# A short convolution with two taps per product in one more channel group, in a fused attention and long-convolution kernel

## The chip, the cores and the metric

The kernel runs on one core of a Trainium2 chip. A core has a matrix engine (TensorE, PE in the profile, with its weight loads as PEld), a vector engine (VectorE, DVE), a scalar engine (ScalarE, ACT), a general engine (GpSimd, POOL) and a synchronisation engine that here issues most of the DMA transfers (SyncE, SP). The metric is the device time of one execution in microseconds.

## The reference

Two independent parts are computed and laid side by side along the last axis: columns 0 to 575 are part A, columns 576 to 1151 are part B. The inputs are bf16, the sequence has 2048 positions and the width is 576.

Part A is attention with a compressive memory: 32 heads of 18 dimensions, 4 segments of 512 positions.

```
for s in range(4):
    logits = einsum('bhqd,bhkd->bhqk', qs, ks) * scale + mask
    a_dot  = softmax(logits) @ vs
    pq     = phi(qs)                      # t + 1 for t > 0, else exp(t)
    a_mem  = (pq @ M) / (pq @ z + 1e-6)
    o      = g * a_mem + (1 - g) * a_dot
    M, z   = M + phi(ks)^T vs, z + sum(phi(ks))
out_a = concat(o) @ wo
```

Part B is a short convolution of k with four taps per channel, a product with v, a long convolution of 2048 positions per channel (by an FFT of 4096 points), a skip term and a product with q.

```
k_shift[s] = sum over i in 0..3 of k[s - i] * shift_k[:, i]
kv         = k_shift * v
y          = irfft(rfft(kv) * rfft(ssm_k)) + kv * ssm_D
out_b      = q * y
```

## The kernel before, in words

**Tiling of part B.** The 576 channels go through in five groups of 128, 128, 128, 128 and 64. The four full groups begin at channels 0, 128, 256 and 384; the last loads channels 448 to 575 and uses the upper 64 of them. For a group, k and v are loaded transposed from HBM (kT, vT: channels on the partitions, 2048 positions along the row, 16 zero columns ahead of k; lines 421 and 424, tag X4 with two slots, X_0 and X_1 in the rows). The four taps of a channel become entries of diagonal weights: `dgf` (lines 432 to 442) builds them, the tile is dg.

For groups 0 to 3 a chunk of 512 positions takes four products of 128x128 weights, one for each tap, each on kT shifted by that many columns and summed in PSUM (`c4`, lines 467 to 470, by way of line 142). For the group in `PAIRED`, which is group 4 alone, one product takes two taps: 64 partitions hold the channels, the other 64 hold the same channels shifted by one position, and the weights have two diagonals of 64 under each other, 128x64. Two such products on the two halves of the columns of the matrix engine make a pair (`cm`, lines 472 to 485, by way of line 144). For group 4 the shifted rows come from one DMA within the tile (`kc4`, line 447), and one more DMA lays the second half of v below the first (`vc`, line 450). VectorE multiplies the PSUM result with v (line 492), a DMA stores it to HBM (kvst, line 498), and the long convolution loads it later in another layout (xsx, line 526): two transform stages, a pointwise product (lines 601 and 606), the inverse, a transposing DMA (zt, line 634), a last stage, the product with q (line 661, tile q, which has one slot) and the output store (line 668).

**Part A.** For every segment the projections of q and k are stored to HBM by DMA (qd, line 1005) and loaded back in an order of 32 rows for each head (pad, line 1019). For every group of four heads there are up to three score products (s0, s1, s2; line 1222), an exponential on ScalarE over 1024 columns at a time (line 1229), a mask on GpSimd (line 1236), the product with v (av), and a passage through HBM (ad, line 1287; am, line 1330) to the memory term and the output projection (stores at line 1379).

**What sets the order.** The work is cut into 1348 named steps (1350 after the change). Three tables, TURN, ENGINE and SLOT, say in what order all steps are issued, on which engine each runs, and which buffer each tile takes; `plan()` decodes them (lines 1412 to 1429), and the loop at lines 1505 and 1506 issues the steps one by one. Each engine goes through its own part of that order strictly in turn: a step that waits holds back everything behind it on the same engine. DMAs are issued from SyncE's queue, a few from ScalarE's. Copies out of PSUM run on ScalarE (line 148) or VectorE (line 150), as the table ENGINE says.

Names as they occur below: conv3.00, conv3.01, conv3.10 and conv3.11 are the four chunks of group 3; kT3 and vT3 its loads; s0_4 is the first score product of the heads' group 4 (the groups of all segments counted through); pad1.0 is the first load of padded rows of segment 1.

Of the kernel before, what the change touches and what calls it, by code (L numbers as in the profile page):

```python
# [1411 lines left out]
def plan(prm=PRM):  # L1412
# [25 lines left out]
    "bQFFBGoBvQAIAUYErgAJAXQECgFLBGwBTARvAXEBbgFqBL4AawBwAfYAUQRSBDwA9AB+AQYA+AD3AKIBBAE9AAEB+QALAVkEWgRNBKQBBgEFAYcBPgA/AAIBBwEYAQMBTgRAABkBGgFCABQBQQBDAB"
    "YAigEVARYB0wBbBAwBRAANARsBdQR7BHYErwBcBNQAEAFrBGwE9QB8BH8BEQESAW0EEwFwBBcBcQRPBFAERQBHACIBcgRzBHcEeAQjASQBeQR6BEYAiAGjAW4EHgEcASABpQEfAV0EbwQdAbAEcwE8"
    "ASEB1wAbACUBbAB1AQ4B2ACJAQ8BXgRyAD0BPgE/AUgASgBmAIMBLgEmATABLwFyAZUESQAnAUsAKgFMAHQBgAGWBIsBTQAsASsBTgBHBIwBMgEzATQBSAR6AdkAOAFSAHwBTwBQAI4B2gB7AW0AjQ"  # L1440
    "E6ATkBVgRVBDUBMQF9AX8EbgA7AYAEXwQpASgBjwEtAY0ElwSYBNsAbwBAATYBSQFgBI4EhAFRAEEBNwHFAcYBQgHHAX0EngFDAVcEfgSTAaABpgRMAVMAggTBAXcBlAHCAcMBlwGBBFgEVABiBJUB"
    "VQCFBNsBmQGbAXkBhgR2AdwB3QGdAVIByQFEAcsBygGWAXgB3gGfAZoBgQGYAU8BoQHTAZwBSAFGAUoByAG1BEsBTQG2BMwB1AHEAY8EUwJSAs0B1QGQBM4BkQFWAM8BVwC3BNAB0QFRAVgAswS4BN"
    "YBtASaBOkBWQBOAUUB0gHqAdcBUwGnBFAB7QHrAUcBYQRWAZAB7wGSAe4BYwGmAbEEZAFXAdgBpwGFAd8BmQThAbIE4AFjBFQCVAGHBKgBiARVAeMBVgLwAVUCWAGpAVcC5AGsBOIB7AHlAagE5gGu"
    "BKoErQSCAakEuQFkBKsErwTnAWUEAwLxAegBBALyAewEmwSDBKoBrQH0AYoEBQKcBIQE/QFYAv8BiQRaApEEugH+AdkB8wEHAlkCCQJbAskECAJZAWkC9QGGAQACXgFaAa4BygSrAV8B9wHiBGAB9g"
    "GvAbYBZgRhAfkBrAFnBGUBkgRbAXIC+wHaAWYBXAH4AQoCuQS6BPoBwQTCBLABLwJoAnQCcQIGAgsC/AEXAnMCwwQMAsQEGAIZAosEAQJ1AiECiQIiAgICIwK7AYwEaARhAr0BEwINAosCvAFjAsYE"
    "FQKxAWkEsgFdAl8C4wR2AhQCDwJcApMEXgIQAm0CHQIRAmoCXQEOArMBngQrArcBYAIkApQEFgIaAh8CHgK4AcUEywTRBGICvgEgAhIC0gTMBHcCegK/AXgCMwIlArkCGwJ5AiYCHAInAigCugLoBO"
    "kEuwKlAowCtAHAAbsEewKOArUBvQKEArwEvwJkAqsChgJlAp0EfAK+AoECjQKtAmYCZwKsAikC5gR+An0CgwKfBI8CrwKxArAC5wSFAoAChwLkBDsCggIqAn8CvgSuAuUEswIsApAC6gSIArQCkQI3"
    "ArUCbgLrBL0EpwKyAtMEOgLxBIoCPAI8A9QE8gS2Au0ELQI9A+4EkwKSAqAEtwLAArwCoQS4AsUCawIyAqQCHgU0Aj0CNQJsAscCxgKaAr8EyQLABMgC8wTKAm8CwQIuAssCwgL0BPUEMALNAvYENg"
    "LPAjgCzAI/AzkCzgJBA9MClALVAtQCPgOiBNACMQLvBKMEzQRCA/AEmwLXAmIBowJaAEADQwJFApwCRAKlBEQDRgLRAtYCXAPZAtgC7QJNAlIDxAKXApUCwwJDA84EZwHSAlsDTgJdA+8ClgLuAkUD"
    "XwPnAukC6AJOA/cE/QRTA9oC8AL4BNsC/gTPBHACpARQA9wC3gLQBKYCXgPHBPEC8wKgAvICRwKYAkYDYAPIBJkCSAPjAk8C6gLkAtUEUAL6BNYEYQMkBd0CRwP/BOUC3wJiA08DAAX0AuEC4AINBU"  # L1450
    "kD4gJRA/UC/QIOBdsE5gKdAkAC9gJBAtcE/wL+AlQD2gT5BPkC6wLYBOwC+wJIAgED+gKhAgIF2QRJAmMDAwMCA2gDogJXAz4CSgM/AgsDngINA2sDTANKAgADDAOfAgcDZwNtA/cCGQP4AmoDaQMB"
    "BQkDSwIIA2wDBAOoAvwCDgOpAg8FCgNlAwcFJQUFAw8DCAUQBSYFBgNkAxADmgPcBGYDqgLdBJwDcwObAxIDEQNuA40DbwNwA3UDcQN6Ax0DWAOWA5gDFQN7Ax8FcgMTA0sDIQMlA30DdAOSA5cDmQ"
    "N3A5QDfANRAgMFTQN5A0ICBAWTA6QDGAN2AxoDVQOdA6YDpQOVA6ADFAOiA3gDHAMWAxsDBQUeA6cDVgOEAxcDngMiBaEDnwMGBSADtAMiAyMFJAMfA/sEtQMmA6MDIwO2A7ADJwP8BLEDIAWoA94E"
# [83 lines left out]
```

## Time and profile before

| | |
|---|---|
| runs | 276.62, 283.88, 286.04 us; median 283.88 |
| profiled execution | 278.62 us, span 276.9 us, mean granted TensorE clock 0.993 |
| TensorE products | 256.1 us busy, 92% of the span |
| VectorE | 235.3 us, 85% |
| ScalarE | 233.9 us, 84% |
| GpSimd | 186.7 us, 67% |
| DMA | 53.96 MB, mean 195 GB/s |

A busy share is an average over the span. The stretches at the beginning and the end have other limits than the middle, so the shares are read together with the table by stretches. A DMA share over 1 in such a table means that the packets of several transfers overlap on the engines. Where a timeline puts several instructions in one row, it gives the start of the first, the time from it to the end of the last, and their count; a few records of products are missing, so a count may be one short.

### The profile page before, as it was taken

Reading aid. Unit: us, or ns where it says so; the run is one execution under the profiler, and the core shown is the slowest. Engines: PE = TensorE matmul, PEld = TensorE weight load, DVE = VectorE, ACT = ScalarE, POOL = GpSimd, SP = SyncE. Lnnn points to the kernel's source line nnn. Section 1 sums busy time; section 2 is a strip of 40 time slices with the busy share of each in tenths; the row PEclk is TensorE's granted clock in tenths of the full one; section 3 lists DMA queues with packets and bytes.
Section 4 is the critical chain, followed back from the end, with each engine's and each line's share of the span. In section 5 each row is a group of like instructions: output and inputs, shape, how many; then the busy total and the mean of one; then the engine's idle time right before and its main releaser. Section 6 shows DMA issues by size and latency. Waiting matters only on the chain. (4 is left out here: it accounts for less than half of the span.)

```text
span 276.9 us, 9623 instructions
## 1 busy us (share of the span) xinstructions
PE 256.1 (92%) x3950; PEld 159.9 (58%) x3961; DVE 235.3 (85%) x380; ACT 233.9 (84%) x293; POOL 186.7 (67%) x266
## 2 busy tenths in 40 slices
PE   5898999999899999999999799999999999789991
PEld 2554666655645666666556466556557665555670
DVE  7788679899999999987989799986898898779942
ACT  4867778888987898989999799999999999799830
POOL 7169324538998968346857799758776499969600
PEclk9999999999999999999999999999999999999997
DMA  6997999998999797997967998688995755586674
GB/s 191 214 160 164 220 241 283 204 217 202 222 190 250 239 179 200 182 241 148 254 156 150 248 203 206 137 213 254 217 208 153 230 179 132 163 196 151 153 134 110
DMA packets 136293, 53.96 MB, mean 195 GB/s; under 512 B 116360, under 2 KB 128952, under 8 KB 136250
## 3 DMA queue, kind: packets, MB, share of 16 engines
q1 hardware_dynamic: 134506, 52.45, 84.6%
q10 hardware_dynamic: 1744, 0.90, 1.2%
q8 instruction: 31, 0.51, 0.8%
q14 instruction: 12, 0.10, 0.1%
HBM read 22.18 MB, written 17.50 MB: 143 GB/s over the span
## 5 line engine op out<-in xcount | busy, mean ns | idle before, releaser
L1229 ACT ACTIVATE P<-PS 128x1024 bf16<-128x1024 f32 x160 | 153.8, 1032 | 14.4 <-PE PS L1222 13.2
L1236 POOL TENSOR_SCALAR_AFFINE_SELECT P<-P 128x512 bf16<-128x512 bf16 (+1 forms) x112 | 80.7, 741 | 53.0 <-ACT P L1229 42.9
L601 POOL TENSOR_TENSOR PQ<-X,Hx 128x256 bf16<-128x256 bf16 x72 | 49.7, 721 | 7.9 <-PE PS L144 4.1
L1222 PE MATMUL PS<-pad 25*128 25x384 bf16 (+6 forms) x512 | 36.5, 300 | 4.0 <-DMA pad<-qk_scratch 1.9
L150 DVE CAST A<-PS 128x1024 bf16<-128x1024 f32 x21 | 25.2, 1218 | 2.4 <-PE PS L144 2.2
L142 PE MATMUL PS<-xT,wk 128*126 128x512 bf16 (+1 forms) x100 | 25.4, 384 | 0.0
L1222 PEld LDWEIGHTS <-pad 25*128 25x128 bf16 (+1 forms) x512 | 11.1, 91 | 24.1 <-issue 17.7
L144 PE MATMUL PS<-P,V 128*32 128x256 bf16 (+3 forms) x512 | 22.9, 302 | 1.3 <-POOL P L1236 1.0
L142 PE MATMUL PS<-xT,wq 128*126 128x512 bf16 (+1 forms) x95 | 24.0, 383 | 0.0
L150 DVE CAST dn<-PS 126x512 bf16<-126x512 f32 (+1 forms) x29 | 19.7, 684 | 4.9 <-DMA qk_scratch<-dn 2.1
L144 PEld LDWEIGHTS <-Ft 128*64 128x64 bf16 x704 | 19.6, 110 | 7.0 <-issue 6.3
L142 PE MATMUL PS<-wv,xT 128*128 128x288 bf16 x160 | 23.5, 287 | 0.0
L142 PE MATMUL PS<-wo,am 126*128 126x288 bf16 (+1 forms) x144 | 22.4, 287 | 1.0 <-ACT P L1229 1.0
L144 PE MATMUL PS<-W,xs 128*64 128x128 bf16 x576 | 21.1, 220 | 1.5 <-ACT P L1229 0.4
L144 PE MATMUL PS<-A,Ft 128*64 128x128 bf16 (+1 forms) x640 | 22.1, 216 | 0.3 <-DVE dn L150 0.2
L144 PEld LDWEIGHTS <-xs 128*64 128x64 bf16 x576 | 18.0, 109 | 6.2 <-issue 5.2
L144 PE MATMUL PS<-G,PQ 64*128 64x128 bf16 (+1 forms) x640 | 20.7, 217 | 0.7 <-ACT P L1229 0.3
L1035 POOL TENSOR_SCALAR f<-dn 126x512 bf16<-126x512 bf16 (+2 forms) x7 | 17.6, 2520 | 4.5 <-ACT dn L148 2.2
L144 PEld LDWEIGHTS <-PQ 64*128 64x128 bf16 (+1 forms) x640 | 18.3, 97 | 3.8 <-issue 2.9
L150 DVE CAST Z<-PS 128x1024 bf16<-128x1024 f32 x13 | 15.9, 1223 | 4.4 <-PE PS L144 2.8
L142 PEld LDWEIGHTS <-xT 128*128 128x128 bf16 x160 | 14.6, 98 | 7.0 <-issue 2.4
L150 DVE CAST X<-PS 128x1024 bf16<-128x1024 f32 x14 | 17.1, 1222 | 1.7 <-PE PS L144 1.2
(165 smaller groups left out, 454.6 us busy)
## 6 DMA issues: line engine op xcount, KB each, us to landing
pad<-qk_scratch SPq DMA_DIRECT2D x15, 512.0 KB
a_scratch<-ou SPq DMA_DIRECT2D x15, 256.0 KB
qk_scratch<-dn SPq DMA_DIRECT2D x15, 252.0 KB
xs<-in_B_ssm_k_dram SPq DMA_DIRECT2D x4, 512.0 KB
kv_scratch<-X SPq DMA_DIRECT2D x4, 512.0 KB
xs<-kv_scratch SPq DMA_DIRECT2D x4, 512.0 KB
q<-in_B_q_dram SPq DMA_DIRECT2D x8, 256.0 KB
out_dram<-q SPq DMA_DIRECT2D x8, 256.0 KB
```

Of the source, the lines that this page charges most:

```text
L142: self.nc.tensor.matmul(out, lhsT=lhsT, rhs=rhs, start=start, stop=stop)
L144: self.nc.tensor.matmul(out, lhsT=lhsT, rhs=rhs, start=start, stop=stop, tile_position=pos)
L150: self.nc.vector.tensor_copy(out=out, in_=in_)
L601: self.nc.gpsimd.tensor_tensor(out=self.t(Pt)[:, 1024 * ri + 256 * k:1024 * ri + 256 * k + 256], in0=a[:, 256 * h:256 * h + 256], in1=self ...
L1035: eng.tensor_scalar(out=self.t(fm)[0:M, ws, :], in0=self.t(dense[m])[0:M, ws, :], scalar1=0.0, scalar2=1.0, op0=ALU.max, op1=ALU.add)
L1222: nc.tensor.matmul(o, lhsT=t[r, 1, q0:q0 + P], rhs=t[r, 0, q0:L], start=True, stop=True, tile_position=(32 * j, 0))
L1229: self.nc.scalar.activation(out=out2(jj), in_=self.psf(pso[jj]), func=ACT.Exp, scale=scale)
L1236: self.nc.gpsimd.affine_select(out=ap, in_=ap, compare_op=ALU.is_ge, fill=0.0, base=0, pattern=pat + [[1, P]], channel_multiplier=-1)
```

## The change

Group 3 (channels 384 to 511) is put into the paired form. It has 128 channels, not 64, so each half of 64 channels needs its own two rows of partitions: for channels 384 to 447 the shifted rows are copied into the upper 64 partitions of kT itself, and for channels 448 to 511, which stood there, both the rows and the shifted rows are first copied into a spare tile, k2, that takes the one slot of tag q. That is two DMAs (kb3, lines 456 and 457) and then one (kc3, line 460), and the second step may not start until the first has read its source. A chunk of 512 positions then takes four products of 128x64 weights, two by two on the two halves of the columns. The code for it is there in the kernel before; the set of groups selects it:

```diff
-PAIRED = (4,)
+PAIRED = (3, 4)
```

The three tables are replaced as a whole. One line of each stands for the rest:

```diff
 TURN = (
-    "AABzAHcAXQACABwAaQADAHUAewB2AIQAYgABAGUAXgBhAIUAjQBkAIcAWwBfAIkAeABjAIsAeQBgAGoAdAAEAAgABQCIAIYAaACMAI4AigAJAB4AXAAfAKkACgAhAAsApQCnAKYADACrAA0AqAAOAI"
...
+    "AABjAGAAdQCGAAEAfQB5AB4AegADAI8AjQCLAAIAXgAEAB8ACABfAGEAZACHAIkAewAFAGoAXQBrACEAIgCIAAkAHAB8AHgAIAAjAI4AdgCQAIoAjABiAAoAbAALAGUAggANAB0AZgCRAJcArQCrAK"
...
```

There are as many weight loads and products on TensorE as before. Some 86 steps change between ScalarE and VectorE, in about equal numbers both ways, and 32 between GpSimd and VectorE. Four loads of attention weights go from ScalarE's queue to SyncE's; one load of weights and two output stores go the other way. SyncE issues four more DMAs in all.

In TensorE's order conv3.00 stood ahead of the score products s1_6 and s0_6 before; it now stands directly behind s0_6, and s2_6 comes between the second and the third chunk. The load pad1.0 stood 68 steps ahead of its reader s1_8 in the whole order and now stands 38 ahead; the load of padded rows for segment 2, pad2.0, stood 33 ahead of its reader s0_17 and now stands 56 ahead.

SyncE's queue from the key load of group 3 to pad1.0, before (X_0 is kT, X_1 is vT; qk_scratch<-dn is a store of projected q and k, a_scratch<-ou and am<-a_scratch belong to the attention's passage through HBM, wo is a weight load):

```order
42 L421 DMA_TRANSPOSE X_0_101<-in_B_k_dram 128x2048
43 L424 DMA_TRANSPOSE X_1_102<-in_B_v_dram 128x2048
44 L526 DMA xs_106<-kv_scratch 128x32x64
45 L1287 DMA a_scratch<-ou_150 128x2x512
46 L1294 DMA cs_157<-ou_150 32x1x128
47 L697 DMA wo<-in_A_wo_dram 126x4x576
48 L1019 DMA pad_123<-qk_scratch_164 128x2x1024
```

and the same stretch of the changed kernel:

```order
42 L421 DMA_TRANSPOSE X_0_101<-in_B_k_dram 128x2048
43 L424 DMA_TRANSPOSE X_1_102<-in_B_v_dram 128x2048
44 L1005 DMA qk_scratch_164<-dn_117 14x9x1024
45 L456 DMA q_104<-X_0_101 64x2048
46 L457 DMA q_104<-X_0_101 64x2048
47 L1005 DMA qk_scratch_164<-dn_116 14x9x1024
48 L1287 DMA a_scratch<-ou_150 128x2x512
49 L1330 DMA am_136<-a_scratch 126x1x512
50 L460 DMA X_0_101<-X_0_101 64x2063
51 L526 DMA xs_105<-in_B_ssm_k_dram 128x32x64
52 L1294 DMA cs_157<-ou_150 32x1x128
53 L1019 DMA pad_123<-qk_scratch_164 128x2x1024
```

The three copies stand behind the value load, with two stores and a load of the attention between the two copies into the spare tile and the one in place; the weight load of wo has gone further back.

ScalarE's queue at the beginning, up to the first exponential (Ft are the tables of the transform, pad and dn the projections of q and k, V those of v, fe the phi of the attention's memory), before:

```order
28 L336 ACTIVATE Ft<-xs_105 128x16x64
29 L148 CAST pad_123<-PS 128x512 x2
30 L148 CAST dn_117<-PS 126x512
31 L336 ACTIVATE Ft<-xs_105 128x16x64
32 L148 CAST V_125<-PS 128x16x2x9
33 L1041 ACT_TABLE_LOAD
34 L1041 ACTIVATE fe_156<-dn_116 126x512
35 L1229 ACTIVATE P_1_132<-PS 128x1024 x2
```

and after the change:

```order
23 L336 ACTIVATE Ft<-xs_105 128x16x64
24 L148 CAST pad_123<-PS 128x512
25 L336 ACTIVATE Ft<-xs_105 128x16x64
26 L1229 ACT_TABLE_LOAD
27 L1229 ACTIVATE P_1_132<-PS 128x1024
28 L1041 ACTIVATE fe_156<-dn_116 126x512
29 L1229 ACTIVATE P_1_132<-PS 128x1024
```

The cast of V and the phi have left the place ahead of the first exponential.

SyncE's queue at the end, from the last transposing load (CT<-Z), before:

```order
191 L634 DMA_TRANSPOSE CT_100<-Z_103 128x32x64
192 L1379 DMA out_dram<-oA_152 128x576
193 L643 DMA q_104<-in_B_q_dram 64x16x64 x2
194 L1379 DMA out_dram<-f_118 128x576
195 L1379 DMA out_dram<-f_119 128x576
196 L1379 DMA out_dram<-oA_151 128x576
197 L668 DMA out_dram<-q_104 64x16x64 x2
198 L1379 DMA out_dram<-f_122 128x576
```

and after the change:

```order
195 L634 DMA_TRANSPOSE CT_100<-Z_103 128x32x64
196 L1379 DMA out_dram<-oA_153 128x576
197 L643 DMA q_104<-in_B_q_dram 64x16x64
198 L1379 DMA out_dram<-oA_152 128x576
199 L1379 DMA out_dram<-oA_151 128x576
200 L643 DMA q_104<-in_B_q_dram 64x16x64
201 L1379 DMA out_dram<-f_121 128x576
202 L1379 DMA out_dram<-f_122 128x576
203 L668 DMA out_dram<-q_104 64x16x64 x2
```

The second q load now has two output stores between it and the first, and no output store of part A stands behind the last stores of part B.

## Rows read from the trace of the kernel before

**Rows 1.** The page, first part: busy us, share of the span, instructions of each engine.

```profile
PE 256.1 (92%) x3950; PEld 159.9 (58%) x3961; DVE 235.3 (85%) x380; ACT 233.9 (84%) x293; POOL 186.7 (67%) x266
```

**Rows 2.** Busy time by stretch; after ACT and POOL: granted clock, DMA share, GB/s.

```profile
0.00:10.00 10.00, 6.14 (x34) 3.17 (x35) 7.88 (x36) 5.99 (x18) 5.03 (x14) 1.00 0.82 216
...
70.00:90.00 20.00, 19.22 (x311) 11.72 (x310) 18.74 (x26) 17.63 (x19) 18.80 (x30) 1.00 1.04 222
...
260.00:277.00 17.00, 10.96 (x116) 7.30 (x115) 8.18 (x15) 4.34 (x10) 2.16 (x4) 0.89 0.63 126
```

**Rows 3.** TensorE's timeline at group 3: start, length, operation, count, idle time before.

```profile
78.69 1.90 PE L142 MATMUL PS<-X,dg 128*128 128x512 bf16 x7
80.52 0.56 PE L1222 MATMUL PS<-pad 25*128 25x384 bf16 x8
...
83.46 0.68 PE L1222 MATMUL PS<-pad 25*128 25x512 bf16 x4
84.30 1.68 PE L142 MATMUL PS<-X,dg 128*128 128x512 bf16 x7 [0.16 <-issue]
85.91 1.07 PE L144 MATMUL PS<-G,PQ 64*128 64x128 bf16 x32
```

**Rows 4.** TensorE's timeline at group 4, which has the paired form.

```profile
108.29 0.62 PE L144 MATMUL PS<-X,dg 128*64 128x512 bf16 x4
108.84 0.41 PE L1222 MATMUL PS<-pad 25*128 25x512 bf16 x4
```

**Rows 5.** SyncE's timeline around the loads of group 3 and the copy of group 4.

```profile
68.84 0.83 SPq L1005 DMA_DIRECT2D qk_scratch<-dn  x1
69.77 4.08 SPq L421 DMA_TRANSPOSE X<-in_B_k_dram  x1
73.96 2.91 SPq L424 DMA_TRANSPOSE X<-in_B_v_dram  x1
...
81.47 0.39 SPq L1019 DMA_DIRECT2D pad<-qk_scratch  x1
...
102.97 0.55 SPq L447 DMA_DIRECT2D X<-X  x1
```

**Rows 6.** Weight loads from the tile of diagonals: ns shortest/median/longest.

```profile
L142 PEld LDWEIGHTS <-dg x64: 95/98/102, 19.1 to 85.4; 128*128 128x128 bf16 x64
...
L144 PEld LDWEIGHTS <-dg x8: 106/106/109, 108.3 to 110.3; 128*64 128x64 bf16 x8
```

**Rows 7.** DMA in the stretch 102 to 108 us, with the issues in it.

```profile
DMA packets 4326, 1.30 MB, mean 216 GB/s; under 512 B 3974, under 2 KB 4170, under 8 KB 4325
...
X<-X SPq DMA_DIRECT2D x1, 257.9 KB
```

**Rows 8.** TensorE's timeline at the score products s0_4 and s1_8.

```profile
69.12 0.60 PE L1222 MATMUL PS<-pad 25*128 25x512 bf16 x4
...
95.16 0.40 PE L1222 MATMUL PS<-pad 25*128 25x384 bf16 x8
```

**Rows 9.** Timelines of SyncE and TensorE at pad2.0 and its reader.

```profile
148.95 0.59 SPq L1019 DMA_DIRECT2D pad<-qk_scratch  x1
...
153.91 0.40 PE L1222 MATMUL PS<-pad 25*128 25x512 bf16 x4 [1.55 <-DMA pad<-qk_scratch]
```

**Rows 10.** The chain that ended last (start, us, what), and SyncE's last issue.

```profile
264.68 0.65 SPq L1379
...
266.18 4.14 DMA q<-in_B_q_dram
...
273.14 0.63 SPq L1379 DMA_DIRECT2D out_dram<-f  x1
```

**Rows 11.** ScalarE's timeline ahead of the first exponential.

```profile
22.34 1.06 ACT L336 ACTIVATE Ft<-xs 128x1024 bf16<-128x1024 int32 x1 [2.23 <-DVE xs L331]
23.31 0.42 ACT L148 CAST V<-PS 128x288 bf16<-128x288 f32 x1
...
25.04 0.63 ACT L1041 ACTIVATE fe<-dn 126x512 bf16<-126x512 bf16 x1
```

More of the change, by code (lines that the diff above doesn't have):

```diff
@@ L1438 @@
[L1438 to L1453, printed above, removed]
@@ new lines @@
+ENGINE = (
+    "AwICAwIBAgMDAgECAQMCAQIBAAIAAgIAAQACAgMEBAQCBAQCAAIAAgACAAIEBAQCAAIAAgACAAIEBAQDAAIAAgACAAIEBAQDBAQAAgACAAIAAgQEBAIEBAACAAIEBAEEAgQEAQIEBAIEBAIDAQQCAA"
+    "ECAwMDAwAAAAAAAAAAAAAAAAQEBAQEAAIAAQABAAEAAQACAAABAgAAAQIAAAICAAACAgQEBAQAAQABAAEAAgQEBAIBAgIBAgIBAgIBAgMBAgAAAgIAAAIBAAACAgAAAgIAAgABAAIAAgACAAIDAAEB"
+    "AwABAQMAAQEDAAEAAQEDAAEBAwACBAQAAQEDAAEBAwABAQMAAgABAQMAAQEDAAIEBAABAQMAAQEDAAEBAwACAAEBAwABAQMAAQQEAAEBAwABAQMAAQEDAAIAAQEDAAEBAwACBAQCAAQCAAQCAAQCAA"
+    "QCAAQCAAIAAgQAAgACBAACAAIEAAIAAgQEBAAAAQEAAAECAAACAgAAAgEAAAICBAQEBAQEBAQEAwECAgECAwECAwECAgECAAABAgAAAgIAAAIBAAACAgACBAQEAAIEAAIEAAIEAAIEAAIEBAQEBAAC"
+    "AwABAQMAAQEDAAEBAwACAAEBAwABAQMAAgQEAAEBAwABAQMAAQEDAAEAAQEDAAEBAwACBAQAAQEDAAEBAwABAQMAAgABAQMAAQEDAAEEBAABAQMAAQEDAAEBAwACAAEBAwABAQMAAgQEAgAEAgMABA"
+    "ICAAQCAwAEAgIABAICAAIAAgQAAgABBAACAAIEAAEAAQQEBAAAAQIAAAIBAAACAgAAAgIAAAECBAQEBAQEBAQEAgECAgECAgECAgECAgECAAACAgAAAQIAAAICAAACAQACBAQEAAIEAAIEAAIEAAIE"
+    "AAIEBAQEBAACAwABAQMAAQEDAAEBAwACAAEBAwABAQMAAgQEAAEBAwABAQMAAQEDAAIAAQEDAAEBAwACBAQAAQEDAAEBAwABAQMAAQABAQMAAQEDAAIEBAABAQMAAQEDAAEBAwABAAEBAwABAQMAAg"
+    "QEAgAEAgIABAIDAAQCAwAEAgMABAICAAEAAgQAAgACBAACAAIEAAIAAgQEBAAAAgIAAAECAAABAgAAAgIAAAICBAQEBAQEBAQEAgECAgECAwECAgECAgECAAACAgAAAgEAAAIBAAABAQACBAQEAAIE"
+    "AAIEAAIEAAIEAAIDAAEAAQABAQMAAQEDAAEBAwACAAEBAwABAQMAAQQEAAEBAwABAQMAAQEDAAIAAQEDAAEBAwACBAQAAQEDAAEBAwABAQMAAgABAQMAAQEDAAIEBAABAQMAAQEDAAEBAwABAAIAAg"
+    "ABAQMAAQEDAAEAAgACAgIABAICAAQCAwAEAgIABAIDAAABAAABBAAAAQAAAgEAAAIAAAEEAAACAAABAQQCAAEAAQACAAEEAAIAAQABAAIAAQACAwIAAgABAAICAgACAAIAAgICAAIAAgACAwIAAQQE"
+    "BAACAAIEBAQCAAIAAgABAAIEAAEAAgABAAIAAQABAwMAAgACAAEDAwACAAIAAQICAAIAAgABAwMAAgQEBAACAAIEBAQCAAIAAgABAAIEAAEAAgABAAIAAQABAwMAAQACAAECAwACAAIAAgMDAAIAAQ"
+    "ABAgIAAgQEBAACAAIEBAQCAAEAAQACAAIEAAEAAgACAAIAAgABAwIAAgACAAICAgACAAIAAQMCAAIAAgABAwIAAgQEBAACAAIEBAQCAAIAAQQAAgABAAIAAgMCAAEAAQABAAICAgABAAEEBAQAAgQE")
@@ new lines @@
+SLOT = (
+    "AAEAAAEAAAAGAAAAAQAEAAEFAAEAAgYHBgABAAMCBgcAAQAABQQFBAEAAAIDAQQABAUBAQIAAgAAAgMHAAYABwUEAwYAAwAABwEEBAACAwEEAAABAgMBAAEAAAIAAQAEAAMABQEBAgIFAwMAAQACBg"
+    "AGBwEABgIGAQQABAQGAgMAAAYDBAIAAgAABgIEAAAGAAMBAQAEBAQAAQQCBgECBgICBAAAAAIGBAACAwcAAgAEAgIGAAMBAQIEBAYEAQAAAAUAAgEDAgIEBQMDAAIBAAQAAgADAQEAAgADAwECAAAB"
+    "BgAGAAEAAAEAAQIAAQADAAAABAABAAQDAQcGAgIBBAYHAAAAAAEBAQUBAwcABAAAAgYABAQCAgIGAAQAAwQABgAAAAYEAwECAAEEAAMAAgQCAQQAAgAGAAIABAICBAQCAAMAAQQAAQQAAAECAAMEAA"
+    "IGAgACAAACBAYEAQMAAAYBBwADAgADAAQEAAcAAgIEAQAFAQYABgAGBwEGAQAHBgEGAQACAAEAAQIAAQAEAAMAAAACAQADAAIDAwAHAgEGAAAABAcBAgYBAwEAAAcBAQAAAgYEAAQAAQAEBAYBBAAC"
+    "BgIDAQAEAgAGBAECBAIGAAIGAwYEBAQAAgQABAMCBgEFAQIEAAQAAgYCAAIEAAAGAgEGAAAEBAYEAwcAAAQBAgADAgQDBgQAAgADAAICAQMCAQcAAAEBAAABBwAHAQAGAQEGAAEAAQIABAABAAMAAA"
+    "AHBAMHAQEGAAYCAgAHAAABAgIBAQEAAwEABAMBAAEABAEGAgIAAQIEAgQAAAUBAAQEBAIDAgEGBAAEAgICAAEDAAQGBAAGAwAEAAECBAACAAIGAQIEBAYEAwIEAAICAAAABgEFAAMAAAMCBgQDBgIE"
+    "AgAAAQcBAAAAAAEBAAQDAAIAAwYAAAYDBAIHAgEBBAEGAgAAAgAEBgAEAQYAAAAABgAEAQEEAAEEAAECBgIEAQEGAAAGBgEGAQAAAgAEAAIGBAQBBgABBAACAgIAAQIEAAQBAAYCAAABAAYAAAQEAA"
+    "QABgACAQQBBAIGBgIEAQAAAAIABAABAgIBAAAAAgYAAgEAAgAAAgYBAAACBAYABgECAAYCAgYAAQAAAAEEAQAABgAGAQECBAEAAAAGAAACBAEGAQYAAgAEBAEEAQECAAQGAgYAAAYAAAAE")
```

50 lines of the change are left out of this document (23 added, 27 removed).

## The prediction

> **What bounds the kernel now.** I began with the page's first part: TensorE is busy 256.1 us of the span of 276.9, ScalarE 233.9 [rows 1]. The windows say where TensorE's other 20.8 us lie. In the first ten microseconds it is idle 3.9 us, in the last 17 us 6.0, and in a stretch of the middle such as 70 to 90 us, where the change sits, 0.8 of 20 us [rows 2]. So over the middle of the span TensorE is the engine that sets the pace: what is taken out of its row there moves everything behind it forward, and what makes it wait there moves everything back. The granted clock is full in that stretch (1.00, that is the level of 2.4 GHz), so no clock term enters. In the same window ScalarE is busy 17.63 of 20 us, and the DMA share is 1.04, so the transfers have no spare room either.
>
> Then come the timelines. The products of channel group 3 stand twice on TensorE's, 1.90 and 1.68 us for seven recorded products each [rows 3] (a record is missing in each; the code issues eight). Group 4 already has the paired form; there one chunk of four products takes 0.62 us [rows 4]. SyncE's timeline shows what the new copies have to be put between [rows 5]: the two transposing loads of the group hold the queue for 4.08 and 2.91 us, and the group 4 copy of nearly the same kind needs 0.55 us to issue.
>
> **The change part by part.** *Products.* Group 3 stays at 16 weight loads and 16 products, but each product has 64 columns and pairs run side by side. By busy time: 1.90 + 1.68 = 3.58 us now, 4 x 0.62 = 2.48 then, so 1.10 us less. By starts: (80.52 - 78.69) + (85.91 - 84.30) = 3.44 us now, 4 x (108.84 - 108.29) = 2.20 then, so 1.24 us less [rows 3, 4]. I take 1.2. The bounds are 0 (no overlap after all; the weight loads that come with the products are no shorter for half the columns, 106 ns against 98 [rows 6]) and half of 3.44, 1.7.
>
> The Trainium skill, "TensorEngine Tiling (Array Packing)", Theoretical Speedup, gives up to 2x for a dimension of 64 or less; by it the term would be 1.7, the upper bound, where the rows of group 4 show 3.44 / 2.20 = 1.56 times. The same page, Key Properties, says that changing the tiling mode drains the engine, which speaks against the change; the idle time of 0.16 us in front of one of the two stretches of whole-array products [rows 3] agrees with some such price, and the paired form has three separate stretches where there were two, so by it the term would be 1.0.
>
> *Weights on the diagonal.* Four builds of 128x64 take the place of four of 128x128 on GpSimd. GpSimd was not full and the builds wait for the key load, not the reverse; I count nothing. The multiply by v and the store are as before, and the store's reader stands far behind it in either order, so nothing there.
>
> *Copies.* Three issues of the kind of the group 4 copy, 3 x 0.55 = 1.65 us of SyncE's queue. Their bytes: one such copy is 257.9 KB, and the stretch that holds it moved 216 GB/s [rows 7], which makes 1.2 us of all DMA engines for each, an estimate of 3.6 us together. When does such a copy land? Not before 1.2 us, and not after 4.75 us, since the group 4 copy had been issued at 103.53 and the product that reads it began at 108.29 [rows 4, 5]; I take 3.0, the middle.
>
> *The wait.* TensorE takes its work in order, and conv3.00 now needs the load, then two copies into the spare tile, then the shift in place, which may not start before the first two have read their source. From the issue of the key load, along SyncE: 4.08 + 2.91 + 0.83 (the q/k store that is issued next) + 1.10 for two copies = 8.92 us; they have landed at 11.92. Behind them on the queue go another q/k store, a store and a load of the attention stage (0.83 + 0.5 + 0.85, the middle one as short as the group 4 copy's issue), to 11.1; so SyncE stands about 0.8 us, issues the shift copy by 12.5, and it lands at 15.5. With the bounds for a landing this is 12.9 or 19.0. On the other side, in the new order conv3.00 stands directly behind the score product s0_6, and the key load is issued before s0_4. In the trace the same six score products, s0_4 to s0_6, take from 69.12 to 83.46 [rows 3, 8], 14.3 us. So TensorE waits 15.5 - 14.3 = 1.2, bounded by 0 and 4.7; I take 1.0, since the load may be issued a little before s0_4. Behind conv3.00 wait two score products and thus the exponentials on ScalarE; GpSimd's mask waits for those.
>
> *The new order.* One wait on TensorE of 1.55 us stands in front of the score product at 153.91, for a load of padded rows issued at 148.95 [rows 9]. In the new order that load has 56 planned steps to its reader instead of 33, so the wait should go; I count half of it, 0.8, for the next late thing is unknown (0 and 1.55 bound it). The load pad1.0, on the other hand, gets 38 steps instead of 68. At the end two more output stores stand ahead of the second q load on SyncE, 2 x 0.65; that load's transfer of 4.14 us is on the chain that ends last. The store that was issued after everything else (0.63) has gone to ScalarE's queue [rows 10]. Between +0.7 and -0.6, I take +0.3.
>
> *The beginning.* In ScalarE's row 2.23 us are idle ahead of the last sine table, and a cast (0.42) and a phi (0.63) run ahead of the first exponential [rows 11]. Both now stand behind it, so the first exponential is 1.05 us earlier at least. TensorE's own row up to there is about as long as before, so I count nothing in the sum and keep it for a rival.
>
> **Sum.** 278.62 (the profiled execution, span 276.9 and 1.7 around it) - 1.2 + 1.0 - 0.8 + 0.3 = 277.9: 0.7 less. The three runs have a median of 283.88, 5.3 above the profiled one, and lie from 276.62 to 286.04; the mean of all four is 281.3. I apply the difference there: 280.6, and say 280.5. Adding the bounds of the four terms gives -1.7 + 0 - 1.55 - 0.6 = -3.9 and 0 + 4.7 + 0 + 0.7 = +5.4: 277 to 287. A measurement of this kernel can tell about 2% from no change.
>
> **Rivals.** *Faster: the whole new order pays.* The products give 1.7, the copies are in time, the wait of 1.55 goes, and the earlier first exponential is carried through: 1.05 from the two steps moved, and up to the idle 2.23 in front of them. TensorE's waits behind the exponentials would shrink by that. 1.7 + 1.55 + 2.4 = 5.7 less: 275.6, that is 2.9% under the median. For it: the new order covers the whole kernel at once, and ScalarE, at 17.63 of 20 us, follows TensorE closely. Against it: the middle has only 0.8 idle us per 20 to give back. Chance 0.31.
>
> *Slower: the copies turn SyncE's queue into the bound.* Place: SyncE between the key load and pad1.0. Price: three issues 1.65, or 2.5 if they are as slow as a q/k store (0.83 each), one stand until the key load has landed and one until the copies have, up to 4.75 together with the first partly covered, about 7 us, and 3.6 us of transfers in a stretch whose DMA share is already 1.04. pad1.0 was issued at 81.47 for a reader at 95.16, 13.7 us [rows 5, 8]; at 38 steps of 68 that is 7.7, and the pad load of rows 9 needed 5.0. So it decides from a delay of 2.7 us: beyond that the score product s1_8 and all exponentials behind it wait. 7 - 2.7 = 4.3 on TensorE, with the transfers' 3.6 on top and the products' gain lost in it: about 7 more, 288. For it: the rows of SyncE are close to each other already. Against it: SyncE can run ahead of TensorE, and has waited for others for part of that time. Chance 0.18.
>
> *The change doesn't do what it says.* The narrow products give nothing: the weight loads, as many as before and no shorter [rows 6], set the pace of the stretch as the products did, and 3.44 us stay. Then the sum is 278.62 + 1.0 - 0.8 + 0.3 = 279.1 with the copies' wait, 281.8 on the other scale: within 2%. The overlap of group 4 (four in 0.62 us [rows 4]) speaks against it. By the Key Properties of the page named above the drain would be its mechanism. Chance 0.10.
>
> **Numbers.** Forecast 0.41, no gain 0.10, so within 2%: 0.51. Faster by over 2%: 0.31. Slower by over 2%: 0.18. The time is 280.5. The range leaves out the far halves of the two outer rivals: 273.5 (below 275.6, by the spread of the shown runs) to 287.5 (just under the slower rival).
>
> **What would show it.** TensorE's stretches of group 3 as four of about 0.6 us instead of 1.90 and 1.68. In front of conv3.00 an idle entry that names the shift copy: 0 to 2 us as forecast, over 4 for the slower rival, where s1_8 would wait for pad1.0 as well. No entry of 1.5 us at s0_17. The first exponential a microsecond or more earlier. If TensorE's busy sum falls by about 1.2 us and its idle time, 20.8 us, stays within 2 of that, I am right; if the idle time changes by 4 us or more either way, the order of issue decided and not the products, and I am wrong.

## The result, and the profile after

The changed kernel took 282.04 us (median of 9 runs, 279.50 to 284.67), the one before 283.88 (9 runs, 276.62 to 286.14). The nine times of before fall into two groups, four of 276.6 to 278.8 us and five of 283.9 to 286.1, and each ratio here compares the faster runs of both kernels: 1.012, 95% interval 1.008 to 1.016. On that footing the change made the kernel slower by about 3 us, where I had forecast 0.7 less. Run once more beside other kernels it had 1.005 (0.999 to 1.011). So it is within the 2% of the forecast, a little on the wrong side of 1, and the sum was wrong by 2 to 4 us.

The first part of the page of the changed kernel, to be laid beside [rows 1]:

```profile
PE 253.8 (90%) x3954; PEld 160.5 (57%) x3961; DVE 236.1 (84%) x390; ACT 233.6 (83%) x290; POOL 180.0 (64%) x254
```

TensorE is busy 2.3 us less than before, and the span is 4.2 us longer, 281.1: idle time grew from 20.8 to 27.3 us. The next two fences say where. Columns as in [rows 2]; first the kernel before, in five of seven stretches:

```profile
0.00:30.00 30.00, 24.70 (x204) 13.42 (x206) 24.24 (x69) 20.36 (x38) 17.18 (x31) 1.00 0.84 196
...
70.00:110.00 40.00, 39.03 (x650) 24.76 (x648) 37.69 (x56) 35.80 (x43) 35.43 (x53) 1.00 0.99 215
110.00:130.00 20.00, 19.19 (x345) 12.39 (x343) 17.67 (x25) 18.57 (x23) 9.03 (x15) 1.00 0.97 195
...
170.00:230.00 60.00, 58.81 (x936) 36.99 (x929) 53.03 (x81) 56.87 (x69) 45.04 (x64) 1.00 0.77 193
230.00:277.00 47.00, 37.72 (x655) 24.49 (x656) 32.26 (x47) 32.28 (x42) 27.70 (x41) 0.96 0.67 153
```

The same stretches of the changed kernel:

```profile
0.00:30.00 30.00, 26.32 (x255) 15.12 (x258) 24.89 (x79) 19.73 (x36) 13.12 (x27) 1.00 0.86 214
...
70.00:110.00 40.00, 35.20 (x588) 22.99 (x588) 34.09 (x57) 37.41 (x45) 30.27 (x37) 1.00 0.93 215
110.00:130.00 20.00, 18.76 (x345) 12.02 (x344) 16.11 (x21) 16.26 (x19) 12.07 (x20) 0.91 1.00 211
...
170.00:230.00 60.00, 55.56 (x892) 35.44 (x894) 53.65 (x82) 53.07 (x65) 37.96 (x54) 1.00 0.78 199
230.00:281.00 51.00, 40.02 (x701) 26.08 (x702) 35.41 (x52) 35.65 (x45) 28.20 (x41) 0.97 0.64 145
```

Up to 30 us TensorE is idle 3.7 us instead of 5.3: the beginning did become faster. From 70 to 110 us, where the copies are and what follows them, it is idle 4.8 us instead of 1.0, and in the 20 us after that the granted clock is 0.91 as a mean. From 170 to 230 us it is idle 4.4 instead of 1.2, and at the end 11.0 instead of 9.3. Not all of this is the pairing's: the order alone, the first experiment, has part of it.

Group 3 on TensorE's timeline of the changed kernel (columns as in [rows 3]; the products on the two halves of the columns are told apart because they read X, which is kT, and q, which is the spare tile):

```profile
81.03 0.38 PE L144 MATMUL PS<-X,dg 128*64 128x512 bf16 x1 [0.44 <-DMA X<-X]
81.03 0.40 PE L144 MATMUL PS<-q,dg 128*64 128x512 bf16 x1
81.24 0.38 PE L144 MATMUL PS<-X,dg 128*64 128x512 bf16 x1
...
82.90 0.38 PE L144 MATMUL PS<-X,dg 128*64 128x512 bf16 x1 [0.41 <-DVE X L492]
...
153.77 0.39 PE L1222 MATMUL PS<-pad 25*128 25x512 bf16 x4
...
209.64 0.40 PE L1222 MATMUL PS<-pad 25*128 25x512 bf16 x4 [1.47 <-DVE oA L150]
```

Two products now start together, at 81.03, and the next pair 0.21 us later: a chunk of two pairs costs 0.43 us, four chunks 1.7 instead of 3.44 [rows 3]. The wait for the shift copy is there, 0.44 us. So is a second one that I had not seen: conv3.10 takes the PSUM slot of conv3.00, and waits 0.41 us for VectorE's multiply. The wait of 1.55 us at s0_17 [rows 9] is gone; its reader starts at 153.77 with none. A new one of 1.47 us stands at 209.64, for a slot that an output evacuation on VectorE has not freed.

SyncE's timeline of the changed kernel, for [rows 5]:

```profile
72.28 0.55 SPq L456 DMA_DIRECT2D q<-X  x1
72.88 1.20 SPq L457 DMA_DIRECT2D q<-X  x1
...
77.50 0.52 SPq L460 DMA_DIRECT2D X<-X  x1
...
82.30 0.37 SPq L1019 DMA_DIRECT2D pad<-qk_scratch  x1
...
98.76 5.59 SPq L450 DMA_DIRECT2D X<-X  x1
...
110.74 3.03 SPq L966 DMA_TRANSPOSE xT<-in_A_x_dram  x1
```

The copies cost the queue 0.55 + 1.20 + 0.52 us, and a stand of 0.9 us ahead of the third. The shift copy, issued by 78.02, is read at 81.03: it landed in at most 3.0 us.

### The profile page after: what moved, and what is told of

Its sections match the earlier page's. It is cut to its first block, busy times and chain, and to the rows that moved or that the text cites. A ratio compares the mean times of both kernels' runs of the same rounds, so it can differ in the third digit from the quotient of the medians.

```text
span 281.1 us, 9615 instructions
## 1 busy us (share of the span) xinstructions
PE 253.8 (90%) x3954; PEld 160.5 (57%) x3961; DVE 236.1 (84%) x390; ACT 233.6 (83%) x290; POOL 180.0 (64%) x254
## 5 line engine op out<-in xcount | busy, mean ns | idle before, releaser
L1236 POOL TENSOR_SCALAR_AFFINE_SELECT P<-P 128x512 bf16<-128x512 bf16 (+1 forms) x112 | 82.2, 753 | 67.2 <-ACT P L1229 50.3
L601 POOL TENSOR_TENSOR PQ<-X,Hx 128x256 bf16<-128x256 bf16 x68 | 45.7, 703 | 6.1 <-PE PS L144 6.1
L1222 PE MATMUL PS<-pad 25*128 25x384 bf16 (+6 forms) x512 | 34.7, 300 | 4.3 <-DMA pad<-qk_scratch 1.7
L150 DVE CAST A<-PS 128x1024 bf16<-128x1024 f32 x20 | 24.2, 1217 | 2.2 <-PE PS L144 1.5
L144 PE MATMUL PS<-W,xs 128*64 128x128 bf16 x576 | 22.0, 225 | 3.5 <-ACT P L1229 1.2
L150 DVE CAST dn<-PS 126x512 bf16<-126x512 f32 (+1 forms) x28 | 19.0, 682 | 7.1 <-PE PS L142 6.3
L144 PE MATMUL PS<-A,Ft 128*64 128x128 bf16 (+1 forms) x640 | 21.1, 216 | 0.9 <-ACT P L1229 0.4
L148 ACT CAST A<-PS 128x1024 bf16<-128x1024 f32 x16 | 15.9, 1024 | 4.8 <-PE PS L144 4.7
L150 DVE CAST Z<-PS 128x1024 bf16<-128x1024 f32 x14 | 17.0, 1213 | 1.3 <-PE PS L144 1.0
L144 PEld LDWEIGHTS <-V 128*32 128x32 bf16 x512 | 11.1, 97 | 11.5 <-issue 2.9
```

What stands on the lines that cost most here:

```text
L144: self.nc.tensor.matmul(out, lhsT=lhsT, rhs=rhs, start=start, stop=stop, tile_position=pos)
L148: self.nc.scalar.copy(out=out, in_=in_)
L150: self.nc.vector.tensor_copy(out=out, in_=in_)
L601: self.nc.gpsimd.tensor_tensor(out=self.t(Pt)[:, 1024 * ri + 256 * k:1024 * ri + 256 * k + 256], in0=a[:, 256 * h:256 * h + 256], in1=self ...
L1222: nc.tensor.matmul(o, lhsT=t[r, 1, q0:q0 + P], rhs=t[r, 0, q0:L], start=True, stop=True, tile_position=(32 * j, 0))
L1236: self.nc.gpsimd.affine_select(out=ap, in_=ap, compare_op=ALU.is_ge, fill=0.0, base=0, pattern=pat + [[1, P]], channel_multiplier=-1)
```

## The experiments

The new order is kept in all of them unless the text says otherwise. Steps are named as above; a line with a minus is the step's old place in the whole order, one with a plus its new place. The kernels of one call ran on one chip, beside runs of before on it.

**The two halves of the change.** The order without the pairing:

```diff
-PAIRED = (3, 4)
+PAIRED = (4,)
-kb3, kc3            (left out of the three tables)
```

> The new order of issue without the paired products in group 3: the three copies are left out of the order, group 3 has its four whole-array products per chunk again, all else stands where the new order puts it. Theory A (the order costs the time: a held DMA queue in front of the attention's loads at 98 to 110 us and a later q load at the end, while the paired products themselves gain about 1.2 us): about 1.2 us more than the changed kernel, ratio to before 1.014 to 1.020. Theory B (the three copies, their queue slots and their bytes cost the time): about the time of before, ratio 0.995 to 1.003.

281.13 us (10 runs), ratio 1.005 (1.002 to 1.009), between the two ranges. So the order alone costs something, about 1.4 us, contrary to the sum; but the paired form on top of it does not bring its 1.2 us either. TensorE of this kernel in two of the stretches, columns as in [rows 2]:

```profile
70.00:110.00 40.00, 37.40 (x596) 23.74 (x592) 34.27 (x58) 37.01 (x45) 30.73 (x38) 1.00 0.91 212
...
170.00:230.00 60.00, 56.38 (x912) 36.13 (x911) 53.37 (x82) 53.09 (x65) 37.80 (x53) 1.00 0.79 198
```

It is idle 2.6 and 3.6 us there, where before has 1.0 and 1.2 and the changed kernel 4.8 and 4.4. So 1.6 of the 3.8 us of new idle time in the first stretch, and 2.4 of the 3.2 in the second, come with the order and need no copy. The wait at s0_17 is gone here too, and others stand in its place: 1.22 us at 138.71 and 1.60 at 169.70 for loads of padded rows, 1.33 at 188.53 and 1.21 at 209.11 for output evacuations on VectorE.

The pairing in the old order:

```diff
 vT3
+kb3
 ...
 wo
+kc3
 pad1.0
-conv3.00 ... conv3.11   (ahead of s1_6 and ahead of s2_6)
+conv3.00 ... conv3.11   (behind s0_6 and around inv0.0 and s2_6)
```

> The old order with the paired products in group 3: the two copies into the spare tile stand behind the value load, the shift copy ahead of pad1.0, and the four chunks of group 3 stand behind s0_6 instead of ahead of it; all else as before. Theory A: a gain of about the products' 1.2 us less a wait of up to 1 us for the shift copy, ratio 0.995 to 1.000. Theory B: the copies delay pad1.0 and what follows on SyncE, ratio 1.008 or more.

292.87 us, ratio 1.047 (1.039 to 1.055). That lies in the open range of Theory B, but the loss is at another place than pad1.0. SyncE and TensorE of that kernel:

```profile
79.11 0.82 SPq L526 DMA_DIRECT2D xs<-kv_scratch  x1
80.02 4.69 SPq L1287 DMA_DIRECT2D a_scratch<-ou  x1
...
85.46 0.46 SPq L697 DMA_DIRECT2D wo<-in_A_wo_dram  x1
86.03 0.48 SPq L460 DMA_DIRECT2D X<-X  x1
```

```profile
92.04 0.64 PE L144 MATMUL PS<-X,dg 128*64 128x512 bf16 x1 [8.21 <-DMA X<-X]
92.04 0.63 PE L144 MATMUL PS<-q,dg 128*64 128x512 bf16 x1
```

The issue behind the 512 KB load is held for 4.69 us, and the shift copy, issued by 86.51 behind the 567 KB of wo, is read only at 92.04: 5.5 us, where the changed kernel needed 3.0 for the same copy. TensorE waited 8.21 us for it, and then ran at the lower of its levels for a while (granted clock 0.50 from 90 to 100 us, the level of 1.2 GHz): the products take 0.63 us here and 0.38 in the changed kernel. Theory A's reading of the pairing alone was wrong: the copy took longer here, with more bytes issued shortly before it. The Trainium skill, "DMA: Bandwidth & Descriptors", Queues, rings and completion order, has it that each DMA engine consumes its descriptors in ring order, and that a transfer's semaphore fires only after every earlier write of that engine; 5.5 us against 3.0 agrees.

**Loads of wo earlier.**

```diff
 pad1.1
+wo, wo4
 kT4
-wo
 cs7, ad7
-wo4
 xsx2, vc
```

> The changed kernel with the two loads of the output weights moved ahead of the key load of group 4 in SyncE's queue, so that they no longer stand directly ahead of the large load of group 2 and the copy vc. Theory A: vc is held 2 to 3 us instead of 5.6, the attention's loads land before VectorE wants them, TensorE's waits of 0.5 and 1.1 us near 110 us and the drop of its granted clock go: 1.5 to 3.5 us less than the changed kernel, ratio to before 1.000 to 1.007. If the hold has nothing to do with the bytes in flight, vc is held as long, ratio 1.012.

282.38 us, ratio 1.007 (1.003 to 1.011): not told apart from the changed kernel. The hold of vc did shrink, from 5.59 us to 2.68, as Theory A said; but with wo in its old place it is 3.92 us in the order alone, 3.95 in the next run, 4.28 in the changed kernel run again and 3.77 with the copies only, so much of the 5.59 was that one profile's. The profiled run, 284.25 us, lost more at a place that the edit does not touch, TensorE's wait for the shift copy:

```profile
84.16 0.38 PE L144 MATMUL PS<-X,dg 128*64 128x512 bf16 x1 [2.17 <-DMA X<-X]
```

With the same order up to there, this wait was 0.44 us in the changed kernel, 0.74 in its second profile and 0.48 in the next run. The hold explains no time that I could measure; that the wait varies by 1.7 us is shown.

**The second q load of the last group early.**

```diff
 q4.0
+q4.1
 oA2.3, oA2.1
-q4.1
```

> The changed kernel with the second q load of the last group put directly behind the first, ahead of two output stores, as it was before. Theory A: the load lands about 2 us earlier, the product with q that ends the chain too: 1.5 to 2 us less than the changed kernel, ratio to before 1.004 to 1.007. Rival (the end is set by the last output projections instead): no change, 1.012.

280.97 us, ratio 0.997 (0.991 to 1.003), more than expected. The ten runs lie from 276.52 to 283.31 us. The end of the chain in the changed kernel, and the product with q on VectorE:

```profile
269.36 2.28 SPq L643
...
271.68 2.91 DMA out_dram<-f
274.59 1.23 DVE q L661
```

The same product with the early load:

```profile
270.57 1.22 DVE L661 TENSOR_TENSOR q<-PS,q 128x1024 bf16<-128x1024 f32 x1 [0.84 <-ACT oA L148]
```

The load went out at 269.36 behind two stores, and was itself held for 2.28 us; VectorE waited until 274.59. (The chain names the transfer that came last before it.) With the load early VectorE waits 0.84 us and for something else. The hold is this one profile's: in the five others with the load at its late place (e1, e3, e5, x1, x2) its issue took 0.63 or 0.64 us. The same edit on the order without pairing:

```diff
-PAIRED = (3, 4)
+PAIRED = (4,)
 q4.0
+q4.1
 oA2.3, oA2.1
-q4.1
```

> The new order without pairing and copies in group 3, with the second q load of the last group directly behind the first. The order alone had 1.005; the early q load should take 1 to 1.7 us off the end: 0.999 to 1.003 under Theory C and D alike. If the end is not set by that load, 1.005.

279.52 us, ratio 0.999 (0.994 to 1.004), against 1.005 without the edit. By the ratios the edit is worth 0.6 to 0.8%, 1.6 to 2.2 us, where the intervals of each pair just touch or overlap. The traces give less. The last transposing load of the changed kernel was issued here:

```profile
262.65 4.04 SPq L634 DMA_TRANSPOSE CT<-Z  x1
```

From there to the end of the span it is 18.4 us (281.1 - 262.65). In the five other traces with the late load the same stretch is 16.6 to 17.4 us, in seven with the early one 15.1 to 16.7, before 15.8. The middles of the two groups, 17.0 and 16.1, are about 1 us apart. In the trace of this run the stretch is 16.7 us and VectorE still waits 1.86 us at the product with q, in that of the order alone 16.9 and 2.00. So the late load costs about 1 us, and with it put right the new order is not measurably slower than before, nor faster.

The changed kernel again, on the chip of that call:

> The changed kernel itself, once more, so that it stands beside the others on one chip. It should have a ratio to before of 1.005 to 1.013. Theory C: its wait for the shift copy at conv3.00 differs from run to run (0.4 us in the first trace, 2.2 in another run of the same order up to there), so its times spread by 2 to 4 us. Theory D (a fixed cost of the new order only): a spread like that of the order alone, about 1.5 us either way.

281.06 us (278.24 to 282.57), ratio 1.005 (0.999 to 1.011). Its spread is 4.3 us, that of the order alone 3.1; but the order with the early q load, which has no copies, spreads by 4.4 (277.64 to 282.02), so the spread does not decide for Theory C. In this profile the wait at conv3.00 is 0.74 us.

**Copies earlier in SyncE's queue.**

```diff
 kT3
+dg3, kb3
 vT3
+kc3
 qd1.1
-kb3
 qd1.0, ad3, am0.0
-kc3
```

and q4.1 early, as above.

> The changed kernel with the three copies placed around the value load (key load, diagonals, two copies, value load, shift copy) instead of behind it and behind two q/k stores, and with the second q load of the last group directly behind the first. Theory C (the pairing saves 1.7 us on TensorE and loses it to the wait for the shift copy, whose landing hangs on the bytes queued ahead of it): no wait at conv3.00, and 1 to 2 us less than the order alone with the same early q load: ratio to before 0.990 to 0.998. Theory D (the copies' bytes and issues delay what follows, wherever they stand): no faster than the order alone with the early q load, 0.998 or more.

283.57 us, ratio 1.015 (1.009 to 1.021): slower than the same with the copies behind the value load (0.997). Theory C failed. The number lies in the open range of Theory D, and what follows on SyncE did come late (pad1.0 at 84.73, 78.28 in the order alone), but less by the copies' issues than by a stand ahead of them. SyncE, then TensorE:

```profile
63.53 4.99 SPq L421 DMA_TRANSPOSE X<-in_B_k_dram  x1
71.92 0.54 SPq L456 DMA_DIRECT2D q<-X  x1
...
77.19 1.79 SPq L1005 DMA_DIRECT2D qk_scratch<-dn  x2
```

```profile
83.24 1.21 PE L1222 MATMUL PS<-pad 25*128 25x512 bf16 x4 [3.38 <-DVE dn L150]
```

SyncE stood from 68.52 to 71.92 until the key load had landed. The copies were then in time, and TensorE had no wait for them. But the two q/k stores came at 77.19 instead of 71.30 and 74.13; I read the wait of 3.38 us for a VectorE cast into the tile dn, which these stores empty, as their lateness passed on.

**The square: products and copies apart.** Products only, on unshifted rows:

```diff
-self.dma("kb%d" % ct, kb, ...)
-self.dma("kc%d" % ct, ka, ...)
-x, w, c0 = k2, 1, 512 * c - 2 * j
+x, w, c0 = kT, 1, 16 + 512 * c - 2 * j
```

> The changed kernel without the three copies: group 3 takes two taps per product, but on rows of kT that nothing has shifted or copied, so the short convolution of group 3 is not computed. With the order alone (neither), the changed kernel (both) and the next run (copies only) it makes the four corners of a square. Theory E (the paired products save 1.7 us on TensorE; the copies give that back, since they make everything behind them on SyncE 2 to 4 us later for some 40 us, which TensorE meets at 100 to 116 us): 1 to 1.7 us less than the order alone (1.005): ratio to before 0.998 to 1.002, no TensorE wait over 0.8 us between 100 and 117 us. Theory F (the products' time was not the limit there; ScalarE or the transfers were): the time of the order alone, 1.004 to 1.006.

280.78 us (12 runs), ratio 1.002 (0.998 to 1.006). TensorE's timeline:

```profile
80.21 1.05 PE L144 MATMUL PS<-X,dg 128*64 128x512 bf16 x8
81.80 0.39 PE L1220 MATMUL PS<-pad 25*128 25x256 bf16 x6 [0.32 <-ACT P L1227]
82.60 0.62 PE L144 MATMUL PS<-X,dg 128*64 128x512 bf16 x4 [0.41 <-DVE X L490]
```

(This kernel is two lines shorter, so its line numbers are two lower.) Of the 1.7 us saved 0.7 come back at once: the score product behind waits 0.32 us for ScalarE to empty its PSUM slots, and the third chunk 0.41 for VectorE. One engine's shorter stretch ran into the two that empty its results.

Copies only, into the spare tile, with whole-array products:

```diff
-PAIRED = (3, 4)
+PAIRED = (4,)
-elif ct in PAIRED:
+elif ct == 3:
-self.q(e).dma_start(out=self.t(kT)[64:128, 1:2064], in_=self.t(kT)[0:64, 0:2063])
+self.q(e).dma_start(out=self.t(k2)[64:128, 0:2047], in_=self.t(kT)[0:64, 0:2047])
```

> The changed kernel with the four whole-array products of group 3 as before, and three copies of the same size in the same places of SyncE's queue, with the same wait of the third for the first, all into the spare tile, which nobody reads. Theory E: SyncE is late by 3 to 4 us at pad1.0 and by 2 to 3 us at the load of x for segment 2, TensorE waits at 100 to 117 us, and the time is 1 to 3 us over the order alone: 1.008 to 1.015. Theory F (the copies fill time in which SyncE had nothing urgent): the time of the order alone, 1.004 to 1.006.

282.14 us, ratio 1.011 (1.005 to 1.017). SyncE of the order alone:

```profile
78.28 0.39 SPq L1019 DMA_DIRECT2D pad<-qk_scratch  x1
...
107.65 2.41 SPq L966 DMA_TRANSPOSE xT<-in_A_x_dram  x1
```

and of the copies only, with TensorE's wait behind it:

```profile
81.38 1.24 SPq L1019 DMA_DIRECT2D pad<-qk_scratch  x1
...
110.17 2.96 SPq L966 DMA_TRANSPOSE xT<-in_A_x_dram  x1
```

```profile
116.79 1.29 PE L142 MATMUL PS<-xT,wq 128*126 128x512 bf16 x5 [1.49 <-DMA xT<-in_A_x_dram]
```

pad1.0 goes out 3.1 us later than in the order alone (in the changed kernel 4.0, at 82.30), and 30 us downstream the load of x for segment 2 is still 2.5 us later (3.1, at 110.74); TensorE waits 1.49 us for it. The order alone has no such wait, nor has it with the early q load or with the products only. This is Theory E, with its numbers. The same wait is 2.02 us in the changed kernel run again, and 1.55 with its q load early:

```profile
116.35 1.29 PE L142 MATMUL PS<-xT,wq 128*126 128x512 bf16 x5 [1.55 <-DMA xT<-in_A_x_dram]
```

In the first profile of the changed kernel it is another load that comes late, that of am, issued at 104.39 (101.10 in the order alone); TensorE waits 0.52 us and then this for VectorE's work on it:

```profile
110.48 0.54 PE L142 MATMUL PS<-rs,selb 128*126 128x128 bf16 x4 [1.10 <-DVE am L1336]
```

The four corners are 1.005 (neither), 1.002 (products), 1.011 (copies), and 1.012 and 1.005 (both, in two calls). Their intervals overlap in part, so no single step from corner to corner is clear of noise; the order of the four agrees with the traces.

**Copies from ScalarE's queue.**

```diff
-self.dma("kb%d" % ct, kb, ..., pk=4096)
+self.dma("kb%d" % ct, kb, ..., pk=4096, queues=("SP", "ACT"))
 eF1x1.0
+kb3                 (on ScalarE)
 exs0_5, phe1.1, exs1_7
+kc3                 (on ScalarE)
```

and q4.1 early.

> The changed kernel with the three copies issued from ScalarE's queue (the two copies behind the evacuation of the first transform's chunk, the shift copy two exponentials later), so that SyncE's queue has the rows of the order alone; and with the second q load of the last group directly behind the first. Theory E: no delay on SyncE, a wait of 0 to 1 us at conv3.00, three issues of about 0.4 us on ScalarE: 0.8 to 1.5 us less than the same kernel with the copies on SyncE (0.997) and than the order with the early q load (0.999): ratio 0.992 to 0.996. Theory F: 0.997 to 1.000, as these.

283.51 us, ratio 1.014 (1.010 to 1.018), outside both ranges. ScalarE and TensorE:

```profile
72.35 1.81 ACTq L457 DMA_DIRECT2D q<-X  x1
74.27 1.94 ACT L1229 ACTIVATE P<-PS 128x1024 bf16<-128x1024 f32 x2 [1.56 <-PE PS L144]
...
78.79 0.47 ACTq L460 DMA_DIRECT2D X<-X  x1
```

```profile
84.15 0.40 PE L144 MATMUL PS<-X,dg 128*64 128x512 bf16 x1 [2.47 <-DMA X<-X]
```

The second issue held ScalarE for 1.81 us and its exponentials with it; and the shift copy took from 79.26 to 84.15, 4.9 us, although nothing of SyncE's stood ahead of it in its queue. The Trainium skill, "DMA: Bandwidth & Descriptors", Queues, rings and completion order, says also that the semaphore waits for earlier writes of a DMA engine across its queues; that would make the other queue no shortcut, and the 4.9 us agree. SyncE was late all the same, with no copy in its queue: pad1.0 at 80.87 (78.28 in the order alone), the load of x at 112.63 (107.65). So this run does not tell the price of the copies' places on SyncE from that of their transfers; that rival is open.

Both q loads of the last group ahead of the last transposing load, on top of it:

```diff
 yo3.0, yo3.1
+q4.0, q4.1
 zt4
-q4.0, q4.1
```

> The run before, with both q loads of the last group ahead of the last transposing load instead of behind it. They have to wait until the output store of the group before has read the tile, which stands directly ahead of them. If the chain at the end is q load, product with q, output store: 1 to 2 us less than the run before (ratio 0.986 to 0.992), and VectorE no longer waits for q at the end. If the transposing load is made as much later: no change.

285.04 us, 1.018 (1.013 to 1.024). The load's wait for the output store came in front of the transposing load, which went out at 268.38 (265.25 in the run before), and TensorE waited 3.68 us for it.

**Pieces of the two orders spliced**, none with pairing in group 3. New order to step 729, then the old:

```diff
 new order, steps 0 to 728
+old order, the steps that are left
```

> The new order for its first 729 steps (to the score product s0_17, 154 us), then the remaining steps in the old order and on the old engines; no pairing in group 3. The order alone was 2.1 us ahead of before at that point of TensorE's work and 1.5 us behind at the end. If the second half of the new order loses those 3.6 us: ratio to before 0.990 to 0.995. If the lead is lost to a limit that both orders have (transfers, ScalarE), it melts in the old order as well: 0.998 to 1.005.

280.72 us, 1.004 (0.999 to 1.009); behind the old second half no lead is left. Old order to step 1201, then the new tail:

```diff
 old order, steps 0 to 1200
+new order, the steps that are left, q4.1 behind q4.0
```

> The old order without pairing in group 3 for its first 1201 steps (about 242 us), then the remaining steps in the new order and on the new engines, with the second q load of the last group directly behind the first. The span behind TensorE's last product of part B's work was 5.8 us in the old tail and 4.1 us in the new one with the early q load. If that is a property of the tail alone: 1 to 1.7 us less than before, ratio 0.994 to 0.997. If the tail's end hangs on what precedes it: 1.000.

280.05 us, 1.004 (1.000 to 1.007): no gain. So the new tail with the early load repairs what the new order broke, and is no gain behind the old one. The new front before the old order, without and with that tail, and a longer one:

```diff
 new order, steps 0 to 92 (in the third run 0 to 203)
+old order                 (in the second and third to step 1200, then the new tail)
```

> The new order for its first 93 steps (some 28 us), then the old order; no pairing in group 3. If the lead of 2.3 us that the new order has on TensorE at 25 us is kept by an order that does not lose it later: ratio 0.991 to 0.995. If a limit behind it (transfers that arrive when they did, exponentials) takes it back in any order: 0.998 to 1.002, with the lead melting within the first 60 us.

> Both together: new front of 93 steps, old order to step 1201, new tail with the early q load; no pairing in group 3. If both are properties of their stretch, the gains add up: 0.985 to 0.992, a version that beats both kernels. If neither is: 1.000.

> As the run before, but with the new order for the first 204 steps (some 47 us). If the lead is safe once made, the time of the run before. If the seam between the orders costs something, it shows at another place than there: within 1 us of it.

1.012 (1.005 to 1.018), 1.015 (1.009 to 1.021) and 1.030 (1.024 to 1.037). The front's lead does not carry over; the third run shows a wait of 4.84 us at 85.08 for a VectorE cast into dn. All three are slower than before, so the seams may cost more than the front gave, and these runs don't say whether a whole order could keep that lead. None of the versions is measurably faster than before.

## Why the prediction was wrong

**The new order: "-0.8" and "+0.3".** These are the terms that failed. Together they make -0.5 us; the order alone measured +1.4 (1.005, 1.002 to 1.009), the one difference among the parts that is clear of noise.

The -0.8 was for the wait at s0_17. It went entirely, 1.55 us, but the order put waits of its own kind in its place: in the order alone 1.22 and 1.60 us for loads of padded rows and 1.33 and 1.21 for output evacuations, in the changed kernel 1.11 at 171.08 for padded rows and 1.47 at 209.64. That the next late thing was unknown was the right caution; halving the term was too little of it.

**"Between +0.7 and -0.6, I take +0.3."** At the end the late q load cost about 1 us in the traces. I priced the two issues ahead of it, 1.3 us, and set the store that left the queue against it, though that store stood behind the end of the chain and shortened nothing.

**The wait of 1.0 us at conv3.00.** It was 0.44 us in the profile, and 0.48, 0.74, 2.17 and 2.47 in others: inside my bounds, and my middle is fair. What failed is that I priced the copies by this wait alone. Their place in SyncE's queue goes with a larger price: everything behind them later by 3 to 4 us, for 30 us, until it met TensorE at the load of x (x2) or at am (the changed kernel). I had this as the slower rival, with a backlog of 7 us and pad1.0 as its place. The mechanism was right, the size 4.0 us, past the 2.7 that I gave as the deciding point, and the place wrong: s1_8 had no wait. My 2.7 was a planned distance, in steps, turned into time. In the order alone pad1.0 goes out at 78.28 and s1_8 starts at 91.66, 13.4 us and not 7.7; with 4.0 us of delay 9.3 are left, more than the 5.0 that the load needs. Copies only cost 0.6% over the order alone, about 1.7 us, with intervals that overlap.

**"TensorE is the engine that sets the pace: what is taken out of its row there moves everything behind it forward."** Half right. The products gained more than I took: 3.44 us became 1.7, so 1.7 less and not 1.2; the start-to-start row of one chunk of group 4 had its two edges in it. The rule of the Trainium skill that I weighed, up to 2x ("TensorEngine Tiling (Array Packing)", Theoretical Speedup), was the better guide here: 3.44 to 1.7 is twice. A price of the change of mode shows in no idle entry of group 3 in this trace apart from the two waits with names. But 0.7 of the 1.7 went straight into two waits for the engines that empty PSUM (x1), and in the time no more than 0.3% is left of it (1.002 against 1.005, not told apart). A busy share of 96% for TensorE in a stretch with ScalarE at 88% and VectorE at 94% [rows 2] should have told me that the next limit is near.

**"I count nothing" for the beginning.** It came, as the faster rival said: in the trace the first exponential starts at 21.46 (25.57 before), and TensorE is idle 1.6 us less up to 30 us. It did not last. By 110 us the 3.8 us of new idle time had eaten it. What kept me from counting it was a correct feeling without a mechanism.

Added up in place of my terms, from the ratios: the order +1.4 us (about 1 of it the q load), the copies +1.7, the products -0.8: +2.3 us, or 0.8%, between the two measurements of 1.2 and 0.5%. The last two are differences of ratios whose intervals overlap; that the sum comes out so near is in part luck. Not settled: how much of the first measurement is the lower granted clock from 110 us on. Three of the nine runs show a mean of 0.988 and took 282.7 to 283.1 us, five others 0.994 to 0.999 and 279.5 to 282.0; but the longest, 284.67 us, has 0.995. The drop is not there in each run, and I could not switch it off alone.
